# Low parts of split operands computed on VectorE instead of GpSimd, with a new table of priorities, in an attention and two feed-forward layers

## The chip, the core and the metric

The kernel runs on one core of a Trainium2 chip. A core has a matrix engine (PE), a vector engine (DVE), a scalar engine (ACT), a general engine (POOL) and a queue engine (SP) that issues transfers. Each engine executes its own list of instructions strictly in the order in which the program wrote them; between engines, semaphores carry the dependences. The metric is the device time of one execution in microseconds (us).

## What is computed

Attention with a memory term over 4 batches of 8 heads, 576 rows and 64 columns a head, then two feed-forward layers over the 2304 resulting rows, all in fp32:

```
scores = scale * q @ k.T, causal; a = softmax(scores); local = a @ v
q_p = phi(q); mem_out = (q_p @ M_prev) / (q_p @ z_prev + 1e-6)
x = g * mem_out + (1 - g) * local            # 2304 x 512
h = x @ w_in;  x = (h * tanh(softplus(h))) @ w_out    # 512 -> 2048 -> 512
h = x @ w_in2; out = (h * sigmoid(h)) @ w_out2        # 512 -> 2048 -> 512
```

## The kernel before

**Attention.** Two heads make a pair; 16 pairs follow one another, with some overlap. For a pair DVE takes scores out of PSUM with a mask and a row minimum (L562), ACT takes the exponential (L586), DVE adds a constant to the row sums and inverts them (L616 and L618, two elements a partition), POOL scales the rows (L601, L619), PE transposes them (L638, L655) and multiplies them with the values (L674), and ACT writes the result into `xT`, which holds all of x with features on partitions (`Vc`, recorded under L481).

**Feed-forward.** Rows go in 6 tiles `t` of 384, the 2048 hidden columns in 16 slices `i` of 128, in 4 groups of 4 slices. One unit is (layer, t, i); there are 192. For a unit PE does 12 matmuls into `hp` (L843 to L845; below, the *in* part), ACT applies the activation (L858) and rounds the result to `gh` (L859), DVE takes the rest `gl = a - gh` (L860), and PE does the *out* part into `acc` (L880; 12 matmuls of 384 columns in layer 0, 9 of 512 in layer 1). After each group of four slices `acc` is added into `xT` (L895 on ACT, L897 on DVE).

**Split operands.** Each fp32 operand of these matmuls is a rounded high part and a low part, original minus high. The high part of x is `xh`, made by ACT (L826); the low part `xl` is made by `lo()` of `split_x` (L829), 4 instructions a tile: 24 in layer 0, 24 in layer 1. A weight slice arrives in `stg` (two buffers); DVE extracts its value in five steps (L761, L769, L771, L773, L776), ACT rounds it (L784) and `s_lo` makes the low part (L788) and frees the `stg` buffer. There are 64 such weight jobs; the 8 of the first group are worked off while attention still runs, the last of them at its end. Before, POOL makes all 64 weight low parts and 46 of the 48 `xl`; DVE makes the other two.

**What sets the order.** The program gives a planner (`Steps.plan`) each step with its engine, an assumed duration and its dependences. The planner works out a latest start for each, adds the sum of the entries of the table `SHIFT` that fit the step, and lists the steps of each engine by walking through an assumed schedule. PE, DVE, ACT, POOL and SP then follow these lists. `PERIOD` spaces the pairs in that schedule. Buffers are rings: 3 banks for `hp`, 5 for `acc`, 3 buffers each for `a`, `gh`, `gl`.

Of the kernel before, what the change touches and what calls it, by code (L numbers as in the profile page):

```python
# [721 lines left out]
GC = NF // NG  # L722
# [5 lines left out]
class Weights:  # L728
# [13 lines left out]
    def steps(self, n):  # L742
        job = self.jobs[n]
        ph, i, part = job
        nc = self.nc

        def s_load():
            t = self.stg.tile([P, DM, 2], I32, tag="stg", name="stg")
            src = self.pairs[ph][part].bitcast(I32)
            if part == 0:  # L750
                nc.sync.dma_start(
                    t.rearrange("p (c f) x -> p c (f x)", c=KC),
                    src[:, 2 * i * P:2 * (i + 1) * P].rearrange("(c p) f -> p c f", p=P))
            else:
                nc.sync.dma_start(t.rearrange("p f x -> p (f x)"), src[i * P:(i + 1) * P, :])
            self.raw[job] = t

        def s_abs():
            c = self.stg.tile([P, DM], F32, tag="val", name="val", bufs=self.VALS)
            self.val[job] = c  # L760
            nc.vector.tensor_scalar(  # L761
                c.bitcast(U32), self.raw[job][:, :, 1].bitcast(U32), 0x7FFFFFFF, None, op0=ALU.bitwise_and)

        def s_bits(n):
            t, c = self.raw[job], self.val[job]
            cu = c.bitcast(U32)
            lo, hi = t[:, :, 0].bitcast(U32), t[:, :, 1].bitcast(U32)
            if n == 0:
                nc.vector.tensor_scalar(c, c, LEAST, MOST, op0=ALU.max, op1=ALU.min)  # L769
            elif n == 1:  # L770
                nc.vector.tensor_scalar(cu, cu, 3, 0x3FFFFFFF, op0=ALU.logical_shift_left, op1=ALU.bitwise_and)  # L771
            elif n == 2:
                nc.vector.scalar_tensor_tensor(  # L773
                    out=cu, in0=lo, scalar=29, in1=cu, op0=ALU.logical_shift_right, op1=ALU.bitwise_or)
            else:
                nc.vector.scalar_tensor_tensor(  # L776
                    out=lo, in0=hi, scalar=0xC0000000, in1=cu, op0=ALU.bitwise_and, op1=ALU.bitwise_or)

        def s_hi():
            k = i % SLOTS  # L780
            pool = self.fix if k < GC else self.late
            w = pool.tile([P, 2, DM], F32R, tag=f"w{k}{part}", name=f"w{k}{part}")
            self.W[job] = w
            nc.scalar.copy(w[:, 0, :], self.raw[job][:, :, 0].bitcast(F32))  # L784

        def s_lo():
            w = self.W[job]
            nc.gpsimd.tensor_tensor(  # L788
                w[:, 1, :], self.raw[job][:, :, 0].bitcast(F32), w[:, 0, :].bitcast(F32), op=ALU.subtract)
        bits = {f"b{n}": lambda n=n: s_bits(n) for n in range(4)}  # L790
        return dict(ld=s_load, abs=s_abs, hi=s_hi, lo=s_lo, **bits)

    def register(self, m, due, last):

        m.cap.update({"W.raw": 2, "W.val": self.VALS})
        for n, job in enumerate(self.jobs):
            ph, i, part = job
            f = self.steps(n)
            k = i % SLOTS
            ring = f"W.{k}{part}"  # L800
            m.cap[ring] = 1
            J = lambda x: ("W", job, x)
            t = due(job)
            slow = 0.2 if ph == 0 and i < GC else 0.0
            for x, e, d, deps in (("ld", "S", 3.8, []), ("abs", "D", 0.465, ["ld"]), ("b0", "D", 0.465, ["abs"]),
                                  ("b1", "D", 0.465, ["b0"]), ("b2", "D", 0.735, ["b1"]), ("b3", "D", 0.78, ["b2"]),
                                  ("hi", "A", 0.57, ["b3"] + (["open1"] if k >= GC else [])),
                                  ("lo", "G", 1.38, ["hi"])):
                m.add(J(x), e, d + (slow if e == "D" else 0.0), [y if y == "open1" else J(y) for y in deps], f[x], t)
            m.hold("W.raw", job, [J("ld")], [J("lo")], order=n)  # L810
            m.hold("W.val", job, [J("abs")], [J("b3")], order=n)
            m.hold(ring, job, [J("hi")], last(job), order=n)


class Moe:
# [5 lines left out]
    def split_x(self, ph, t, kc):  # L821
        nc = self.nc
        ts = slice(t * TB, (t + 1) * TB)

        def hi():
            nc.scalar.copy(self.xh[t][:, kc], self.xT[:, kc, ts])  # L826

        def lo():
            self.lo_engine(ph, t, kc).tensor_tensor(  # L829
                self.xl[t][:, kc], self.xT[:, kc, ts], self.xh[t][:, kc].bitcast(F32), op=ALU.subtract)  # L830
        return hi, lo

# [67 lines left out]
        r = t * TB + d * P  # L900
        self.nc.sync.dma_start(self.out[r:r + P, :], self.part(1, t, d))

    def lo_engine(self, ph, t, kc):
        return self.nc.vector if ph == 0 and t == 0 and kc % 2 else self.nc.gpsimd

    def open(self, n):

        tc, ctx = self.tc, self.ctx
# [17 lines left out]
    def register(self, m, base, ends, step=4.17):  # L926
# [6 lines left out]
        for t in range(NB):  # L933
            for kc in range(KC):
                k = ("x", t, kc)
                f = self.split_x(0, t, kc)
                heads = [(b * KC + kc, v) for b in range(t * TB // SEQ, ((t + 1) * TB - 1) // SEQ + 1) for v in ends]
                m.add((k, "h"), "A", 0.413, ["open%d" % (t // 3)] + heads, f[0], due[0, t, 0])
                e = self.lo_engine(0, t, kc) is self.nc.gpsimd
                m.add((k, "l"), "G" if e else "D", 0.955 if e else 0.466, [(k, "h")], f[1], due[0, t, 0])  # L940
        for n, u in enumerate(U):
            ph, t, i = u
            g = i // GC
# [26 lines left out]
            if i % GC == GC - 1:  # L970
                for d in range(nd):
# [11 lines left out]
                    if g == NG - 1 and ph == 0:  # L983
                        f = self.split_x(1, t, d)
                        z = ("z", t, d)
                        m.add((z, "h"), "A", 0.413, [k], f[0], due[1, t, 0])
                        m.add((z, "l"), "G", 0.955, [(z, "h")], f[1], due[1, t, 0])
                    elif g == NG - 1:
                        m.add((k, "st"), "S", 0.5, [k], lambda t=t, d=d: self.store(t, d), due[u] + 4)

# [10 lines left out]
        self.w.register(m, wdue, wlast)  # L1001


PERIOD = 9.921
SHIFT = {
# [19 lines left out]
}  # L1025


# [75 lines left out]
```

## Time and profile before

| | |
|---|---|
| median of 3 runs | 1046.67 us (1046.45 to 1046.94) |
| profiled execution, its own time | 1046.64 us |
| its span, first to last instruction | 1044.8 us |
| PE, share of the span busy | 97% |
| DVE | 56% |
| ACT | 44% |
| POOL | 28% |

The profiled time is within 0.03 us of the median, and 1.84 us of it lie outside the span. A busy PE in this profile is not PE at its peak: matmuls overlap, and one row of 0.33 us follows the one before it after 0.17 us. So idle time of PE alone undercounts what a stall costs, and the pace (how far apart the rows start) is the better measure.

### The profile page before, as it was taken

The page shows a single profiled execution, that of the slowest core. Times are in us where ns is not written, and L with a number is a line of the kernel's source. Part 1 is how long each engine was busy: PE and PEld are TensorE (multiplying, and loading weights), DVE is VectorE, ACT ScalarE, POOL GpSimd, SP SyncE. Part 2 cuts the span into 40 slices and gives each one's busy share as a digit, 9 for nine tenths or more (in the row PEclk, how much of TensorE's full clock was granted, in tenths as well). Part 3 has the DMA queues.
Part 4 walks back from the last instruction along what each step waited for, and adds up shares of the span by engine and source line. Part 5 has one row for each costly group of instructions (what it writes and reads, how often), then busy time and mean ns, then how long its engine had stood idle before and what let it go on. Part 6 is the DMA issues. An engine that isn't in the chain of part 4 may idle for free.

```text
span 1044.8 us, 15751 instructions
## 1 busy us (share of the span) xinstructions
PE 1015.3 (97%) x5824; PEld 902.3 (86%) x5824; DVE 584.3 (56%) x1398; ACT 461.5 (44%) x1071; POOL 291.6 (28%) x303
## 2 busy tenths in 40 slices
PE   6999999988999999999999999999999999999998
PEld 4666666677999999999999999899999999998897
DVE  6999999999724732672278238512752372212222
ACT  6899898983424322332234334324422332222221
POOL 4887778787201200210024234101200120000000
PEclk9999999999999999999999999999999999999999
DMA  6433343122302300220031002100300120000011
GB/s 135 101 92 82 92 102 93 46 67 68 102 1 61 101 1 1 82 81 1 1 101 61 1 21 81 61 1 21 118 24 1 41 81 1 1 1 31 31 61 61
DMA packets 85309, 55.03 MB, mean 53 GB/s; under 512 B 61936, under 2 KB 78320, under 8 KB 85232
## 3 DMA queue, kind: packets, MB, share of 16 engines
q1 hardware_dynamic: 84032, 53.73, 18.2%
q8 instruction: 46, 0.75, 0.3%
q10 hardware_dynamic: 1200, 0.30, 0.1%
q14 instruction: 31, 0.25, 0.1%
HBM read 49.29 MB, written 4.72 MB: 52 GB/s over the span
## 4 chain that ended last, share of the span: by engine, by line
PE 80%; DVE 10%; POOL 4%; ACT 3%; issue 2%; DMA 1%; SPq 0%; POOLq 0%; ACTq 0%; DVEq 0%
PE acc L880 37%; PE hp L843 12%; PE hp L844 12%; PE hp L845 12%; DVE sm L562 3%; POOL xl L829 2%; PE ps_x L674 2%; PE ps_s L569 2%; DVE h L484 2%; ACT P L586 2%; PE ps_t L638 1%; DVE z L616 1%; DVE e L513 1%; PE ps_t L489 1%; DMA nq<-in_q_dram 1%
## 5 line engine op out<-in xcount | busy, mean ns | idle before, releaser
L858 ACT ACTIVATE a<-hp 128x384 f32<-128x384 f32 x192 | 94.5, 492 | 469.5 <-PE hp L845 469.4
L860 DVE TENSOR_TENSOR gl<-a,gh 128x384 fp32r<-128x384 f32 x192 | 116.4, 606 | 320.6 <-ACT gh L859 320.1
L843 PE MATMUL hp<-xh,w 128*128 128x384 f32 x768 | 258.9, 337 | 0.0
L844 PE MATMUL hp<-xl,w 128*128 128x384 f32 x768 | 258.5, 337 | 0.0
L845 PE MATMUL hp<-xh,w 128*128 128x384 f32 x768 | 258.5, 337 | 0.0
L788 POOL TENSOR_TENSOR w<-stg,w 128x512 fp32r<-128x512 f32 x64 | 86.6, 1354 | 474.5 <-ACT w L784 341.1
L880 PE MATMUL acc<-gh,w 128*128 128x384 f32 x768 | 212.1, 337 | 1.5 <-ACT gh L859 1.5
L880 PE MATMUL acc<-w,gh 128*128 128x512 f32 x576 | 180.4, 394 | 0.0
L843 PEld LDWEIGHTS hp<-xh,w 128*128 128x128 f32 x768 | 144.2, 188 | 4.5 <-issue 0.3
L844 PEld LDWEIGHTS hp<-xl,w 128*128 128x128 f32 x768 | 144.2, 188 | 4.2 <-DVE xl L829 0.2
L845 PEld LDWEIGHTS hp<-xh,w 128*128 128x128 f32 x768 | 144.2, 188 | 0.0
L880 PEld LDWEIGHTS acc<-gh,w 128*128 128x128 f32 x768 | 140.6, 188 | 1.8 <-ACT gh L859 1.8
L880 PE MATMUL acc<-gl,w 128*128 128x384 f32 x384 | 130.2, 339 | 7.0 <-DVE gl L860 7.0
L880 PEld LDWEIGHTS acc<-w,gh 128*128 128x128 f32 x576 | 106.9, 188 | 17.4
L897 DVE TENSOR_TENSOR xT<-acc,xT 128x384 f32<-128x384 f32 (+1 forms) x126 | 73.9, 612 | 83.6 <-PE acc L880 83.6
L880 PE MATMUL acc<-w,gl 128*128 128x512 f32 x288 | 113.8, 395 | 0.2 <-DVE gl L860 0.2
L601 POOL TENSOR_SCALAR P<-P,z,g 128x448 f32<-128x448 f32 (+3 forms) x128 | 94.0, 746 | 31.1 <-DVE z L618 17.3
L859 ACT CAST gh<-a 128x384 fp32r<-128x384 f32 x192 | 98.6, 513 | 5.4
L586 ACT ACTIVATE P<-sm,m 128x576 f32<-128x576 f32 (+4 forms) x144 | 83.7, 583 | 8.8 <-DVE m L562 6.7
L880 PEld LDWEIGHTS acc<-gl,w 128*128 128x128 f32 x384 | 72.1, 188 | 9.5 <-DVE gl L860 9.4
L784 ACT CAST w<-stg 128x512 fp32r<-128x512 f32 x64 | 42.3, 661 | 68.9 <-DVE stg L776 62.3
L880 PEld LDWEIGHTS acc<-w,gl 128*128 128x128 f32 x288 | 54.1, 188 | 14.0 <-DVE gl L860 1.4
(80 smaller groups left out, 1131.2 us busy)
## 6 DMA issues: line engine op xcount, KB each, us to landing
stg<-in_moe_w_in_dram SPq DMA_DIRECT2D x32, 512.0 KB, 3.7
stg<-in_moe_w_out_dram SPq DMA_DIRECT2D x32, 512.0 KB, 3.5
out_dram<-xT SPq DMA_DIRECT2D x18, 256.0 KB, 2.0
nq<-in_q_dram SPq DMA_DIRECT2D x32, 128.0 KB, 2.6
nv<-in_v_dram SPq DMA_DIRECT2D x32, 128.0 KB, 2.7
nk<-in_k_dram SPq DMA_DIRECT2D x30, 128.0 KB, 2.7
z<-in_z_prev_dram SPq DMA_DIRECT2D x4, 256.0 KB, 4.4
nq<-in_q_dram SPq DMA_DIRECT2D x16, 32.0 KB, 2.5
```

The source lines that it names most:

```text
L586: nc.scalar.activation(G(f"P{i}")[:, 1 - j if i else 1], s[f"sm{i}{j}"], AF.Exp, bias=s[f"m{i}"][:, j:j + 1], scale=-1.0, accum_out=G(f"z{ ...
L601: f[f"n{i}{j}"] = lambda i=i, j=j: nc.gpsimd.tensor_scalar(s[f"P{i}"][:, 1 - j], s[f"P{i}"][:, 1 - j], s[f"z{i}"][:, j:j + 1], self.g1[:, ...
L784: nc.scalar.copy(w[:, 0, :], self.raw[job][:, :, 0].bitcast(F32))
L788: nc.gpsimd.tensor_tensor(w[:, 1, :], self.raw[job][:, :, 0].bitcast(F32), w[:, 0, :].bitcast(F32), op=ALU.subtract)
L843: nc.tensor.matmul(hp, lhsT=wh, rhs=xh, start=(kc == 0), stop=False)
L844: nc.tensor.matmul(hp, lhsT=wh, rhs=xl, start=False, stop=False)
L845: nc.tensor.matmul(hp, lhsT=wl, rhs=xh, start=False, stop=(kc == KC - 1))
L858: f["si"] = lambda: nc.scalar.activation(self.new(u, "a", TB), self.hp[u], fn)
L859: f["gh"] = lambda: nc.scalar.copy(self.new(u, "gh", TB, F32R), g("a"))
L860: f["gl"] = lambda: nc.vector.tensor_tensor(self.new(u, "gl", TB, F32R), g("a"), g("gh").bitcast(F32), op=ALU.subtract)
L880: nc.tensor.matmul(o, lhsT=a, rhs=b, start=(first and k == 0), stop=(last and k == 2))
L897: nc.vector.tensor_tensor(part, acc, part, op=ALU.add)
```

## The change

Three things. Every `xl` is computed by DVE (`lo_engine` is gone). `s_lo` runs on POOL only for the first group of layer 0 (8 jobs), on DVE for the other 56. The planner is told so, with 0.466 and 0.6 as the assumed durations on DVE. The table of priorities is another one, and has entries for classes of steps that had none: the parts of a feed-forward unit by layer (`M`), the drains (`dr`), the weights by group (`Wg`) and by group, slice and part (`Wj`), and the second layer's splits (`z`). No instruction is added or dropped.

```
         def s_lo():
             w = self.W[job]
-            nc.gpsimd.tensor_tensor(
+            eng = nc.gpsimd if ph == 0 and i < GC else nc.vector
+            eng.tensor_tensor(
                 w[:, 1, :], self.raw[job][:, :, 0].bitcast(F32), w[:, 0, :].bitcast(F32), op=ALU.subtract)
...
         def lo():
-            self.lo_engine(ph, t, kc).tensor_tensor(
+            nc.vector.tensor_tensor(
                 self.xl[t][:, kc], self.xT[:, kc, ts], self.xh[t][:, kc].bitcast(F32), op=ALU.subtract)
...
-    def lo_engine(self, ph, t, kc):
-        return self.nc.vector if ph == 0 and t == 0 and kc % 2 else self.nc.gpsimd
...
-PERIOD = 9.921
+PERIOD = 10.582
 SHIFT = {
-    ('a', 'ldnk'): 25.36, ('a', 'ldnv'): 49.95, ('a', 'phe'): -177.34, ('a', 'phu'): -13.77, ('a', 'Tk'): 18.81,
...
+    ('a', 'ldnk'): 30.28, ('a', 'ldnv'): 61.83, ('a', 'phe'): -269.17, ('a', 'phu'): -0.59, ('a', 'Tk'): 15.94,
...
```

How the lists change is shown at three places. In the names, `w_...` is a weight slice, `xl_...` the low part of one tile of rows, `P_...` a score block; numbers differ between the two programs.

POOL, at the end of attention, before; `w_3532` is the sixth of the first group's eight weight slices, `w_3627` and `w_3707` the seventh and eighth, `w_3781` the first of the next group:

```order
L788 TENSOR_TENSOR w_3532<-stg,w_3532 128x512
L601 TENSOR_SCALAR P_3446<-P_3446,z_3447,g_105 128x320
L829 TENSOR_TENSOR xl_3588<-xT,xh_3587 128x384 x2
L788 TENSOR_TENSOR w_3627<-stg,w_3627 128x512
L829 TENSOR_TENSOR xl_3590<-xT,xh_3589 128x384 x4
L829 TENSOR_TENSOR xl_3592<-xT,xh_3591 128x384
L788 TENSOR_TENSOR w_3707<-stg,w_3707 128x512
L829 TENSOR_TENSOR xl_3592<-xT,xh_3591 128x384 x3
L829 TENSOR_TENSOR xl_3685<-xT,xh_3684 128x384
L788 TENSOR_TENSOR w_3781<-stg,w_3781 128x512
```

The same place in the changed program, down to POOL's last computing instruction:

```order
L789 TENSOR_TENSOR w_3528<-stg,w_3528 128x512
L619 TENSOR_SCALAR P_3504<-P_3504,z_3505,g1s 128x128
L601 TENSOR_SCALAR P_3472<-P_3472,z_3473,g_105 128x192
L601 TENSOR_SCALAR P_3437<-P_3437,z_3438,g_105 128x320
L789 TENSOR_TENSOR w_3652<-stg,w_3652 128x512
L789 TENSOR_TENSOR w_3752<-stg,w_3752 128x512
```

POOL's list ends with the last two weight slices of the first group; all `xl` and all later weight slices are gone from it.

DVE, where the feed-forward begins, before, from the last steps of attention's end to the second `gl`:

```order
L829 TENSOR_TENSOR xl_3588<-xT,xh_3587 128x384
L769 TENSOR_SCALAR val<-val 128x512
L771 TENSOR_SCALAR val<-val 128x512
L773 SCALAR_TENSOR_TENSOR val<-stg,val 128x512
L776 SCALAR_TENSOR_TENSOR stg<-stg,val 128x512
L761 TENSOR_SCALAR val<-stg 128x512
L860 TENSOR_TENSOR gl<-a,gh 128x384
L769 TENSOR_SCALAR val<-val 128x512
L771 TENSOR_SCALAR val<-val 128x512
L860 TENSOR_TENSOR gl<-a,gh 128x384
```

The changed program, around its first three `gl`:

```order
L773 SCALAR_TENSOR_TENSOR val<-stg,val 128x512
L830 TENSOR_TENSOR xl_3678<-xT,xh_3677 128x384
L776 SCALAR_TENSOR_TENSOR stg<-stg,val 128x512
L830 TENSOR_TENSOR xl_3678<-xT,xh_3677 128x384 x3
L761 TENSOR_SCALAR val<-stg 128x512
L830 TENSOR_TENSOR xl_3680<-xT,xh_3679 128x384
L861 TENSOR_TENSOR gl<-a,gh 128x384 x3
L769 TENSOR_SCALAR val<-val 128x512
L830 TENSOR_TENSOR xl_3680<-xT,xh_3679 128x384
L771 TENSOR_SCALAR val<-val 128x512
L830 TENSOR_TENSOR xl_3680<-xT,xh_3679 128x384 x2
```

The `xl` now stand between the weight steps; 17 of the first layer's 24 come ahead of the first `gl`, which itself comes after more of the weight work than before.

PE, at the first out part, before; `w_3162` is the third slice for the *in* part of the first tile, `w_1663` the first slice for the *out* part:

```order
L845 MATMUL hp<-xh_3587,w_3162 128x384
L880 MATMUL acc<-gh,w_1663 128x384
L880 MATMUL acc<-gl,w_1663 128x384
L880 MATMUL acc<-gh,w_1663 128x384 x2
```

The changed program at its first out part; `xh_3588` is the second tile of rows, `w_2247` the second slice, `w_1661` the first slice for the *out* part:

```order
L846 MATMUL hp<-xh_3588,w_2247 128x384
L881 MATMUL acc<-gh,w_1661 128x384
L881 MATMUL acc<-gl,w_1661 128x384
L881 MATMUL acc<-gh,w_1661 128x384 x2
```

Before, PE's list has three *in* parts, two *out* parts, and then alternates, so that one unit is in hand between its *in* and its *out* part. Changed, it has six *in* parts, three *out* parts, and then alternates with three units in hand, from the second half of the first layer on with two.

## Rows read from the trace of the kernel before

**Rows 1.** The page, part 1: busy us, share of the span, instructions.

```profile
PE 1015.3 (97%) x5824; PEld 902.3 (86%) x5824; DVE 584.3 (56%) x1398; ACT 461.5 (44%) x1071; POOL 291.6 (28%) x303
```

**Rows 2.** Busy time by stretch: length, busy us (instructions) by engine, clock, DMA.

```profile
25.00:222.00 197.00, 189.30 (x1413) 125.01 (x1411) 189.37 (x720) 176.78 (x500) 149.59 (x174) 1.00 0.36 86
...
230.40:270.00 39.60, 31.12 (x169) 29.04 (x169) 35.72 (x39) 18.33 (x41) 26.66 (x21) 1.00 0.26 79
...
300.00:650.00 350.00, 350.00 (x1997) 348.48 (x1995) 177.08 (x295) 118.29 (x232) 65.95 (x53) 1.00 0.14 44
```

**Rows 3.** The chain that ended last, from 222 us: start, us, what.

```profile
225.08 5.07 POOL xl L829 x4
...
272.24 2.08 PE acc L880 x12
```

**Rows 4.** PE in time order: the first feed-forward matmuls, and the last.

```profile
222.11 0.45 PE L843 MATMUL hp<-xh,w 128*128 128x384 f32 x1
...
223.38 0.76 PE L674 MATMUL ps_x<-W,MV 128*64 128x320 f32 x4
...
224.72 0.44 PE L843 MATMUL hp<-xh,w 128*128 128x384 f32 x1
...
1040.78 0.40 PE L880 MATMUL acc<-w,gl 128*128 128x512 f32 x1
```

**Rows 5.** PE's matmuls from 222 to 272.2 us by form: count, busy, mean ns.

```profile
L880 PE MATMUL acc<-gh,w 128*128 128x384 f32 x65 | 17.9, 337 | 1.5 <-ACT gh L859 1.5
L843 PE MATMUL hp<-xh,w 128*128 128x384 f32 x40 | 13.6, 340 | 0.0
...
L880 PE MATMUL acc<-gl,w 128*128 128x384 f32 x32 | 11.5, 358 | 7.0 <-DVE gl L860 7.0
```

**Rows 6.** PE's weight loads from 222 to 272 us: who waited for whom, us, times, longest.

```profile
PEld acc L880 <- DVE gl L860: 9.1, 7, 2.9
PEld acc L880 <- ACT gh L859: 1.8, 1, 1.8
```

**Rows 7.** The same from 272 us to the end.

```profile
PEld acc L880 <- DVE gl L860: 1.7, 4, 0.6
```

**Rows 8.** DVE in time order, 219 to 270 us: start, duration, instruction.

```profile
219.62 1.38 DVE L776 SCALAR_TENSOR_TENSOR stg<-stg,val 128x512 uint32<-128x512 uint32 x1
220.92 0.68 DVE L484 COPY h<-ps_t 128x512 f32<-128x512 f32 x1
221.52 1.26 DVE L829 TENSOR_TENSOR xl<-xT,xh 128x384 fp32r<-128x384 f32 x1
...
263.14 0.43 DVE L771 TENSOR_SCALAR val<-val 128x512 uint32<-128x512 uint32 x1
263.60 0.69 DVE L773 SCALAR_TENSOR_TENSOR val<-stg,val 128x512 uint32<-128x512 uint32 x1
264.40 0.69 DVE L776 SCALAR_TENSOR_TENSOR stg<-stg,val 128x512 uint32<-128x512 uint32 x1
...
267.38 0.55 DVE L860 TENSOR_TENSOR gl<-a,gh 128x384 fp32r<-128x384 f32 x1
267.85 0.41 DVE L769 TENSOR_SCALAR val<-val 128x512 f32<-128x512 f32 x1
```

**Rows 9.** `gl` from 230 to 265 us, then from 300 to 400: min/median/max ns.

```profile
L860 DVE TENSOR_TENSOR gl<-a,gh x7: 546/1342/1371, 231.8 to 261.9; 128x384 fp32r<-128x384 f32 x7
...
L860 DVE TENSOR_TENSOR gl<-a,gh x24: 548/558/1367, 303.2 to 399.1; 128x384 fp32r<-128x384 f32 x24
```

**Rows 10.** `xl`: two on POOL in time order; POOL's from 222 to 262 us; DVE's two.

```profile
219.15 1.30 POOL L829 TENSOR_TENSOR xl<-xT,xh 128x384 fp32r<-128x384 f32 x1
221.36 1.01 POOL L829 TENSOR_TENSOR xl<-xT,xh 128x384 fp32r<-128x384 f32 x1 [0.91 <-ACT xh L826]
...
L829 POOL TENSOR_TENSOR xl<-xT,xh 128x384 fp32r<-128x384 f32 x21 | 25.9, 1262 | 0.9 <-ACT xh L826 0.9
...
L829 DVE TENSOR_TENSOR xl<-xT,xh 128x384 fp32r<-128x384 f32 x2 | 2.6, 1318 | 0.0
```

**Rows 11.** Attention's additions to the row sums, 25 to 222 us, ns and totals.

```profile
L616 DVE TENSOR_SCALAR z<-z x74: 107/162/1527, 26.4 to 213.7; 128x2 f32<-128x2 f32 x60, 128x1 f32<-128x1 f32 x14
...
L616 DVE TENSOR_SCALAR z<-z 128x2 f32<-128x2 f32 (+1 forms) x74 | 21.8, 296 | 2.5 <-ACT P L586 2.0
```

More of the change, by code (lines that the diff above doesn't have):

```diff
@@ L807, in register @@
                                   ("hi", "A", 0.57, ["b3"] + (["open1"] if k >= GC else [])),
-                                  ("lo", "G", 1.38, ["hi"])):
+                                  ("lo",) + (("G", 1.38) if ph == 0 and i < GC else ("D", 0.6)) + (["hi"],)):
                 m.add(J(x), e, d + (slow if e == "D" else 0.0), [y if y == "open1" else J(y) for y in deps], f[x], t)
@@ L938, in register @@
                 m.add((k, "h"), "A", 0.413, ["open%d" % (t // 3)] + heads, f[0], due[0, t, 0])
-                e = self.lo_engine(0, t, kc) is self.nc.gpsimd
-                m.add((k, "l"), "G" if e else "D", 0.955 if e else 0.466, [(k, "h")], f[1], due[0, t, 0])
+                m.add((k, "l"), "D", 0.466, [(k, "h")], f[1], due[0, t, 0])
         for n, u in enumerate(U):
@@ L986, in register @@
                         m.add((z, "h"), "A", 0.413, [k], f[0], due[1, t, 0])
-                        m.add((z, "l"), "G", 0.955, [(z, "h")], f[1], due[1, t, 0])
+                        m.add((z, "l"), "D", 0.466, [(z, "h")], f[1], due[1, t, 0])
                     elif g == NG - 1:
```

57 rows, old and new, of the table SHIFT are left out of this document.

## Prediction

> **What bounds the kernel now.** I read the page's busy shares first [rows 1]: PE is at 97%, so only the stretches in which PE is not fed can give anything. The busy times by stretch [rows 2] show where: in the feed-forwards (300 to 650 us) PE is busy all the time while DVE has half of it free; from 230.4 to 270 us PE works only 31.12 of 39.60 us, with DVE at 35.72; in attention (25 to 222 us) PE and DVE are both at 96%. The chain of waits [rows 3] runs through POOL's `xl` (the row at 225.08 us is the first of several such) and from 272.24 us, where the row stands for all that follow, through PE alone. So the place of this change is 222 to 270 us, where attention hands over to the feed-forward. Everything behind it is PE at its pace, and a microsecond saved there is a microsecond at the end.
>
> What the handover costs is read from PE's pace. From the first feed-forward matmul at 222.11 [rows 4] to 272.24 [rows 3] PE did 10 *in* parts (40 matmuls of L843, four a part) and 8 *out* parts (64 with `gh` and 32 with `gl`, twelve a part; the 65th opens the next) [rows 5]. Undisturbed, a part takes 2.08 us (the row at 272.24 [rows 3]), and attention's last product in between takes 224.72 - 223.38 = 1.34 us [rows 4]. That makes 18 x 2.08 + 1.34 = 38.8 us; it took 50.1. So 11.3 us were lost. The waits of PE's weight loads give nearly the same, with names: 9.1 us for DVE's `gl`, 1.8 us for ACT's `gh`, together 10.9 [rows 6]. I use 10.9.
>
> Why `gl` is late there: DVE is slowed. The same instruction takes 1.342 us at the median in that stretch and 0.558 us later [rows 9]; L776 takes 1.38 us at 219.62, while POOL makes an `xl` (219.15 to 220.45), and 0.69 us at 264.40, with none on POOL [rows 8, 10]. 21 `xl` on POOL, 1.262 us each [rows 10], thus hold back about as many DVE instructions by 0.7 to 0.8 us each.
>
> **The change part by part.**
>
> *The first layer's `xl` (22 more on DVE, all in the handover).* The price of one on DVE without POOL beside it is not in the trace. The two DVE rows have 1.318 us [rows 10], but the one shown (221.52, 1.26 us [rows 8]) stands beside a POOL `xl` (from 221.36). Same engine, operation, shape and types are in `gl` at 267.38: 0.55 us, the next instruction 0.47 us after it [rows 8]. I take 0.47; the bounds are 0.47 and 1.26. On DVE the whole list from the seventh weight slice's last step (L776) to the first `gl` is: 17 `xl`, one copy of 0.6, four weight steps of 0.46, one of 0.80, one of 0.7 [rows 8]: 8.0 + 0.6 + 1.8 + 0.8 + 0.7 = 11.9 us. POOL still makes one weight slice in that time: one collision, 1.38 - 0.69 = 0.7. It begins where L484 begins at 220.92 [rows 8], less the 0.7 that L776 lost there to a POOL `xl` that is gone: 220.2. So the first `gl` can start at about 232.8. PE, from 222.11, has six *in* parts ahead of its first *out* part: 222.11 + 1.34 + 6 x 2.08 = 235.9. `gl` is there 3 us before it is wanted. Before, three *in* parts stood ahead, so by its pace PE would have come to its first *out* part at 229.7, and the first `gl` began at 231.8 [rows 9].
>
> The first matmul needs the first two `xl`: 220.2 + 2 x 0.47 = 221.1, ahead of 222.11. I credit no earlier start; that could be up to 1 us. What stays lost: the split first unit, and short waits for ACT, which has all of the 24 roundings `xh` earlier in its list than before. Between 0.3 and 3 us; I take 0.8, since each single wait for ACT now is at most 1.8 and the buffers of `hp` cover three units. **Handover: -10.9 + 0.8 = -10.1 us.**
>
> *The 56 weight low parts and the second layer's 24 `xl` on DVE.* 56 x about 0.7 (the weight form is 512 columns wide; L773 with two inputs of that width takes 0.69) + 24 x 0.55 = 52 us more on DVE, spread over 770 us, where DVE is idle about half the time [rows 2]. They lie beside PE's work. The cost if that cover is gone: a low part stands right behind its own last step L776 in places, so DVE waits for ACT's rounding, under 1 us, with `gl` queued behind it, and PE waits for `gl`. PE now has two or three units in hand, 8 to 12 us, so I cost it at nothing. The load of the weight slice after next is issued when a low part is done; on SP nothing stands behind it that PE waits for. Two of these loads also move behind the transfers of an attention pair; at nothing, for weight slices are wanted long after. In return the collisions with POOL end here too: of the 1.7 us that weight loads still wait for `gl` after 272 us [rows 7] I take back 1.3. **Feed-forwards: -1.3 us** (0 to -1.7; +2 if DVE's in-order waits reach PE now and then).
>
> *The new priorities in attention.* The same instructions on the same engines, in another order for about half of them. POOL's work there is the same. Both lists have six of the first group's weight slices begun on DVE before the last score block. What the order can change is how often DVE runs into POOL: the 74 additions to row sums take 0.162 us at the median and 0.296 on average, up to 1.527 [rows 11], which makes 21.8 - 74 x 0.162 = 9.8 us of collisions. DVE is at 96% there, so most of it counts. I see nothing that moves this one way; I take 0, with 4 us (40% of those 9.8) to either side.
>
> *The tail* (last drain, last store) is the same on all engines: 0.
>
> **Sum:** 1046.64 (the profiled execution, 0.03 below the median) - 10.1 - 1.3 + 0 = 1035.2 us, 1.1% faster.
>
> **The rivals.**
>
> *A. An `xl` on DVE costs 1.26 us with POOL idle too.* Then 17 x (1.26 - 0.47) = 13.4 us come on DVE ahead of the first `gl`: 232.8 + 13.4 = 246.2, against 235.9, so PE waits 10.3 us, and the total is 1035.2 + 10.3 = 1045.5: no change. For it speaks that the only two DVE rows have that price; against it that `gl`, the same form, takes 0.55 as soon as POOL is quiet. The Trainium skill points this way: its page "Perfetto Trace Analysis", section "Optimizing Scalar/DVE Operations", says that DVE and POOL share a read port, so moving work between the two might not help. Followed to the letter it would leave the handover as it is, about 1046 us. The rows do not bear it out: per `xl` POOL's 1.262 us stand against 0.55 on DVE. Chance 4%.
>
> *B. Attention gets slower by more than the handover wins.* One mechanism: DVE's additions to row sums, or POOL's scalings, meet each other more often. A full hit costs 1.527 - 0.162 = 1.37 us; the 9.8 us are about 7 such hits in 197 us. To be slower than before by 0.2% (2.1 us) the new order needs (11.4 + 2.1) / 1.37, about 10 more hits, all on the path: 17 instead of 7. It would end near 1049. Chance 4%. A part of that, 4 to 9 us, gives 1040 to 1044.5, still faster: 11%.
>
> *C. Attention gets faster* by the same mechanism, more than 4 us: below 1031. Chance 9%.
>
> *D. The change does not do what it says* (low parts still on POOL): the lists exclude it; POOL's ends with attention.
>
> **How the numbers follow.** The forecast, 1031 to 1040, has 72%, A 4%, B 4%, its milder form 11%, C 9%. The predicted time is 1035.2. The range, 1030.5 to 1042.5, takes in the bounds of the handover (2.2 above, 0.5 below, 1 for an earlier start) and of attention (4 either way); about 7% lie below it and 13% above. About 0.2%, or 2.1 us, is what a measurement of this kernel tells from no change: faster 92% (forecast, milder B, C), same 4% (A), slower 4% (B).
>
> **What would show it.** In the changed profile: POOL has no row behind attention's end, and its busy time falls from 291.6 us by over 100; `xl` on DVE has a mean near 0.6, and `gl` a median near 0.56 from 225 to 270 us too; PE's weight loads wait about 1 us instead of 10.9 in the 50 us behind the first feed-forward matmul; that matmul starts within 4 us of 222.1; from there PE keeps its parts 2.08 us apart at once. The first matmul's start tells attention's share, the distance from there to the last matmul (818.7 us before [rows 4]) the handover's and the feed-forwards'; that distance should be about 807. I am wrong if the distance shrinks by much less than 11 us (A, or waits of DVE for ACT), or if the start moves by more than 4 us (B or C).

## The result, and the profile after

The changed kernel takes **1033.15 us** (median of 4 runs, 1033.11 to 1033.78) against 1046.8 us beside it: ratio **0.987**, 95% interval [0.985, 0.989]. The prediction was 1035.2 us with a range of 1030.5 to 1042.5; the time is 2 us below the forecast and inside the range. The profiled execution took 1033.11 us.

The first look is at the busy shares and at the stretches that [rows 1] and [rows 2] showed of before (stretch, length, then busy us with instructions of PE, its weight loads, DVE, ACT and POOL, then the granted clock, the share of the DMA engines and GB/s):

```profile
PE 1010.8 (98%) x5824; PEld 901.8 (87%) x5824; DVE 584.1 (57%) x1500; ACT 461.1 (45%) x1071; POOL 160.7 (16%) x201
```

```profile
25.00:222.00 197.00, 189.10 (x1420) 124.49 (x1420) 189.23 (x724) 178.58 (x505) 146.30 (x172) 1.00 0.37 86
222.00:272.00 50.00, 50.00 (x293) 49.42 (x290) 42.22 (x84) 29.40 (x62) 3.08 (x2) 1.00 0.28 89
230.40:270.00 39.60, 39.60 (x230) 39.60 (x229) 32.04 (x64) 20.52 (x43) 1.32 (x1) 1.00 0.29 93
300.00:650.00 350.00, 350.00 (x1990) 348.04 (x1990) 192.39 (x363) 119.47 (x235) 0.00 (x0) 1.00 0.15 47
```

DVE has 102 instructions more and yet the same busy time (584.1 us, before 584.3): what 102 more rows cost it, the rows that POOL no longer holds up gave back. From 230.4 to 270 us PE works 39.60 of 39.60 us, before 31.12. The rows of PE's weight loads that waited for `gl` and `gh` [rows 6, 7] have no counterpart: not one such wait is left.

PE in time order gives the two parts of the account (first feed-forward matmul, the first *out* part, the last matmul; start, duration):

```profile
220.39 0.42 PE L844 MATMUL hp<-xh,w 128*128 128x384 f32 x1
...
234.64 0.33 PE L881 MATMUL acc<-gh,w 128*128 128x384 f32 x1
234.81 0.33 PE L881 MATMUL acc<-gl,w 128*128 128x384 f32 x1
...
1027.24 0.40 PE L881 MATMUL acc<-w,gl 128*128 128x512 f32 x1
```

Against [rows 4] the first matmul comes 222.11 - 220.39 = **1.72 us earlier** (attention's share), and the distance from it to the last one falls from 818.67 to 806.85 us, by **11.82 us** (handover and feed-forwards). I call these two numbers *start* and *distance* from here on. Behind the first *out* part the chain of waits holds PE alone, with twelve matmuls in the undisturbed 2.08 us from the start:

```profile
234.80 6.24 PE acc L881 x36
...
243.12 2.08 PE acc L881 x12
```

DVE at the handover, in time order, answers [rows 8], and the two groups of `gl` (min/median/max ns) answer [rows 9]:

```profile
218.91 1.54 DVE L830 TENSOR_TENSOR xl<-xT,xh 128x384 fp32r<-128x384 f32 x3
...
222.89 0.55 DVE L830 TENSOR_TENSOR xl<-xT,xh 128x384 fp32r<-128x384 f32 x1
223.36 1.55 DVE L771 TENSOR_SCALAR val<-val 128x512 uint32<-128x512 uint32 x1
...
231.06 0.55 DVE L830 TENSOR_TENSOR xl<-xT,xh 128x384 fp32r<-128x384 f32 x1
233.28 1.50 DVE L861 TENSOR_TENSOR gl<-a,gh 128x384 fp32r<-128x384 f32 x3 [1.67 <-ACT gh L860]
```

```profile
L861 DVE TENSOR_TENSOR gl<-a,gh x11: 551/558/559, 233.3 to 262.8; 128x384 fp32r<-128x384 f32 x11
L861 DVE TENSOR_TENSOR gl<-a,gh x179: 548/558/561, 275.1 to 1022.4; 128x384 fp32r<-128x384 f32 x179
```

An `xl` takes 0.55 us on DVE; one row at 223.36 stands beside a POOL row and takes 1.55 instead of 0.42. Two weight slices are all that POOL still makes behind the first feed-forward matmul (the 3.08 us of the second stretch above). The first `gl` waited 1.67 us, not for DVE but for ACT's `gh`.

Attention's additions to the row sums [rows 11] took 18.7 us, 3.1 less than before:

```profile
L616 DVE TENSOR_SCALAR z<-z 128x2 f32<-128x2 f32 (+1 forms) x74 | 18.7, 255 | 1.2 <-ACT P L586 0.8
```

### The profile page after: what moved, and what is told of

Its sections match the earlier page's. It is cut to its first block, busy times and chain, and to the rows that moved or that the text cites. A ratio compares the mean times of both kernels' runs of the same rounds, so it can differ in the third digit from the quotient of the medians.

```text
span 1031.3 us, 15634 instructions
## 1 busy us (share of the span) xinstructions
PE 1010.8 (98%) x5824; PEld 901.8 (87%) x5824; DVE 584.1 (57%) x1500; ACT 461.1 (45%) x1071; POOL 160.7 (16%) x201
## 4 chain that ended last, share of the span: by engine, by line
PE 88%; DVE 8%; ACT 2%; DMA 1%; POOL 1%; issue 1%; SPq 0%; ACTq 0%; POOLq 0%
PE acc L881 39%; PE hp L844 13%; PE hp L846 13%; PE hp L845 13%; PE ps_x L674 3%; PE ps_s L569 3%; PE ps_t L638 2%; DVE sm L562 2%; DVE h L484 2%; PE ps_t L489 1%; DVE z L616 1%; ACT P L586 1%; DMA nq<-in_q_dram 1%; DVE e L513 1%; POOL P L601 1%
## 5 line engine op out<-in xcount | busy, mean ns | idle before, releaser
L861 DVE TENSOR_TENSOR gl<-a,gh 128x384 fp32r<-128x384 f32 x192 | 106.8, 557 | 308.4 <-ACT gh L860 307.1
L601 POOL TENSOR_SCALAR P<-P,z,g 128x576 f32<-128x576 f32 (+3 forms) x128 | 93.2, 739 | 36.8 <-ACT P L586 8.1
L586 ACT ACTIVATE P<-sm,m 128x448 f32<-128x448 f32 (+4 forms) x144 | 83.8, 584 | 6.7 <-DVE m L562 5.3
L638 PEld LDWEIGHTS ps_t<-ident,P 128*128 128x128 f32 x384 | 41.5, 141 | 25.3 <-POOL P L601 6.2
L569 PE MATMUL ps_s<-kT,qT 64*128 64x288 f32 (+3 forms) x320 | 62.8, 473 | 0.4 <-DVE m L562 0.3
```

Of the source, the lines that this page charges most:

```text
L569: nc.tensor.matmul(ps, lhsT=s["qT"][R[j], qcols(i)], rhs=s["kT"][R[j], k0 + cols.start:k0 + cols.stop], start=True, stop=True)
L586: nc.scalar.activation(G(f"P{i}")[:, 1 - j if i else 1], s[f"sm{i}{j}"], AF.Exp, bias=s[f"m{i}"][:, j:j + 1], scale=-1.0, accum_out=G(f"z{ ...
L601: f[f"n{i}{j}"] = lambda i=i, j=j: nc.gpsimd.tensor_scalar(s[f"P{i}"][:, 1 - j], s[f"P{i}"][:, 1 - j], s[f"z{i}"][:, j:j + 1], self.g1[:, ...
L638: nc.tensor.transpose(ps[:, o:o + P], src, self.ident)
L861: f["gl"] = lambda: nc.vector.tensor_tensor(self.new(u, "gl", TB, F32R), g("a"), g("gh").bitcast(F32), op=ALU.subtract)
```

## Experiments

Two theories stood against each other. **Theory 1:** DVE was slowed by POOL's rows beside it; take them away and `gl` is in time, the units that PE has in hand being a reserve. **Rival 2:** the new order, with three units in hand instead of one, is the gain, and which engine makes the low parts matters little. A second pair concerns attention: **theory B**, that the row-sum additions and their collisions lie on its path, against the view that PE or the list sets its pace. Lists are those of before or after, as each edit says. All were compared with the kernel before, which took 1046.8 to 1047.0 us at the median beside them.

### The engines without the new priorities

```
-PERIOD = 10.582
+PERIOD = 9.921
 SHIFT = {
-    ...            # the new table
+    ...            # the table of before
```

> The changed kernel's engines with the table of priorities and the period of before: PE's list again has three in parts ahead of its first out part and one unit in hand. Theory 1 (what made PE wait was that POOL's low parts slowed DVE; the units in hand are a reserve that is hardly drawn on): almost all of the gain between the first feed-forward matmul and the last stays, their distance is 807 to 809 us (818.7 before, 806.9 changed), and the time is 1035 to 1037 us, the rest being the later start. Rival 2 (the units in hand, so the table, made the gain): the distance is 815 us or more, the time 1043 or more.

Measured: 1035.87 us (1035.64 to 1035.91), ratio 0.990 [0.988, 0.991]. Start 222.28, distance 807.73. PE has three *in* parts and two *out* parts ahead of the alternation, as before: one unit in hand. This is all that waits for `gl` or `gh` behind it:

```profile
PEld acc L881 <- DVE gl L861: 1.2, 1, 1.2
```

The change of engines alone brings 10.94 of the 11.82 us of distance and nothing of the start. The new table brings the other 0.88 us and the whole of the start.

### The new lists with POOL's `xl`

```
+            eng = nc.gpsimd if ph == 0 and not (t == 0 and kc % 2) else nc.vector
-            nc.vector.tensor_tensor(
+            eng.tensor_tensor(
                 self.xl[t][:, kc], ...
```

> The changed kernel with every list as it is, except that the first layer's 22 low parts of x that POOL made before are made by POOL again, each at its place in the program's order. PE keeps six in parts ahead and three units in hand. Theory 1: DVE is slowed again in the handover, gl takes 1.3 us there, PE waits 5 to 10 us for gl, time 1038 to 1043 us. Rival 2: the three units in hand cover DVE's slowness, gl still takes 1.3 us but PE waits under 2 us, time 1033 to 1035.5 us.

Measured: 1039.12 us (1038.54 to 1040.08), ratio 0.993 [0.991, 0.994]. Start 220.60, distance 812.07: 5.2 us worse than after, but 6.6 better than before. PE's weight loads from 216 to 272 us, and ACT in time order at the stall:

```profile
PEld acc L882 <- ACT xT L897: 3.6, 1, 3.6
...
PEld acc L882 <- DVE gl L862: 0.3, 1, 0.3
```

```profile
251.55 0.66 ACT L784 CAST w<-stg 128x512 fp32r<-128x512 f32 x1 [6.37 <-DVE stg L776]
252.10 0.86 ACT L897 COPY xT<-acc 128x384 f32<-128x384 f32 x2
```

The time fell into theory 1's range, but not by the wait it names. Three units in hand did cover `gl`: 0.3 us instead of 9.1. The slowed DVE reached PE another way: ACT stood 6.37 us in front of a weight rounding whose last step was late on DVE, and the drain that PE needed to get its `acc` bank back stood behind it in ACT's list. Both theories hold a part: 6.6 us are gained although POOL makes the first layer's `xl`. That is the new lists together with the weights' low parts and the second layer's `xl`, which stay on DVE here; how much of it is the lists alone no run shows, for none has the new lists with all of POOL's rows.

### The old lists with the first layer's `xl` on DVE

```
-            self.lo_engine(ph, t, kc).tensor_tensor(
+            (nc.vector if ph == 0 else nc.gpsimd).tensor_tensor(
```

> The kernel before with every list as it is, except that the first layer's 22 low parts of x on POOL go to DVE, each at its place in the program's order. PE has one unit in hand as before. Theory 1: gl takes 0.56 us in the handover, PE's weight loads wait 1 to 3 us there instead of 10.9, time 1036 to 1039 us. Rival 2: DVE is free of collisions, but with one unit in hand PE still waits 7 us or more, time 1043 us or more.

Measured: 1039.39 us (1039.06 to 1039.81), ratio 0.993 [0.992, 0.995], a little above theory 1's range. Start 222.10, distance 810.66: these 22 instructions alone bring 8.0 us. Left are 3.4 us of waits for `gl` in the handover and 1.3 behind it, since POOL still makes the weights' low parts and PE has one unit in hand.

### The weights' low parts on POOL, all 64

```
-            eng = nc.gpsimd if ph == 0 and i < GC else nc.vector
+            eng = nc.gpsimd
```

> The changed kernel, with all 64 low parts of weights on POOL at their places in the lists (before the change that engine made them too); the low parts of x stay on DVE. It asks what the 56 low parts of weights contribute by themselves. Theory 1 (once the low parts of x are off POOL, PE has three units in hand and a lone collision of DVE with POOL is covered): no weight load of PE waits for gl after the first out part, gl still has single rows near 1.3 us, 1033 to 1034.2 us. Rival 2 (each collision that is left reaches PE through an engine's list): 1034.5 to 1036 us, with waits of 1 to 3 us in all at PE's weight loads behind the handover.

Measured: 1033.51 us (1032.88 to 1033.83), ratio 0.987 [0.986, 0.989], as theory 1 expected. Start 220.90, distance 806.85, which is after's to the hundredth. Single rows of `gl` still take 1.35 us in the handover and up to 1.43 later (median 0.56), and none makes PE wait. So moving 56 of the 64 low parts of weights brought nothing here. With one unit in hand the same rows on POOL cost 810.66 - 807.73 = 2.9 us; that comparison also moves the second layer's `xl`, and the planner's lists with them.

### One unit in hand, by a ring of two in the planner

```
-        m.cap.update({"M.h": 3, "M.y": 5})
+        m.cap.update({"M.h": 3, "M.y": 5, "M.hand": 2})
...
+            m.hold("M.hand", u, [N("in") if n else N("in0")], outs, order=n)
```

> The changed kernel with one more rule for the planner: at most two units between their in and their out part, so that PE's list is two in parts, then alternating, with one unit in hand; engines and table as changed. Theory 1 as it stands in the prediction's sum has DVE's first gl behind 17 low parts and the weight steps: gl ready near 231 to 232 us, while PE would come to its first out part at 220.4 + 1.3 + 4.2 = 226 us; so 5 to 6 us lost once at the start of the feed-forward and under 1 us after, time 1037.5 to 1040 us. Rival 2: a loss of 8 us or more, spread over several units, 1041 us or more. If one unit in hand is enough: 1033 to 1034.5.

Measured: 1042.60 us (1041.93 to 1042.88), ratio 0.996 [0.995, 0.997]; theory 1 missed, the time lies where rival 2 put it. Start 221.09, distance 815.60. The waits, and the stretches around them (PE, its weight loads, DVE, ACT, POOL, clock):

```profile
PEld acc L881 <- ACT gh L860: 6.8, 1, 6.8
PEld acc L881 <- DVE gl L861: 0.7, 1, 0.7
```

```profile
226.00:232.00 6.00, 1.09 (x7) 0.77 (x5) 5.83 (x13) 5.97 (x13) 0.00 (x0) 0.94 0.30 87
232.00:236.00 4.00, 2.14 (x6) 1.75 (x7) 2.44 (x5) 1.94 (x5) 1.30 (x1) 0.50 0.08 23
236.00:240.00 4.00, 4.00 (x19) 4.00 (x19) 4.00 (x10) 0.68 (x1) 0.00 (x0) 0.73 0.28 113
```

PE did not wait for `gl` but for `gh`. ACT was busy 5.97 of 6.00 us: the changed priorities put eight roundings `xh` and a weight rounding between the activation and its `gh`. So this run does not price a missing unit in hand; it shows what happens when ACT's list is not in step with PE's. The price of one unit in hand with an ACT list that fits is the first experiment's 0.88 us. Of the 8.75 us of distance lost here the two waits make 7.5; the clock fell too, of which more below.

### A twin of each `xl` on POOL

```
+            if ph == 0:
+                nc.gpsimd.tensor_tensor(
+                    self.twin[t // 3], self.xT[:, kc, ts], self.xh[t][:, kc].bitcast(F32), op=ALU.subtract)
             nc.vector.tensor_tensor(
                 self.xl[t][:, kc], ...
```

> The changed kernel, and for each of the first layer's xl also a twin of it on POOL, which writes a buffer that nobody reads (24 POOL instructions more; the output is that of the changed kernel). No data comes later by the twins themselves, so it prices POOL's presence beside DVE alone. Theory 1 (DVE is slowed by POOL's row, not late by waiting for POOL's results): DVE's rows beside the twins take about 1.3 us instead of 0.55 to 0.7, some 20 of them before the first gl, which comes near 245 us instead of 233; PE stalls of 8 us or more, 1041 to 1048 us. Rival 2 (what cost time before was DVE and PE waiting for POOL's results, not the slowed rows): at most 1036 us.

Measured: 1047.96 us (1047.56 to 1048.86), ratio 1.001 [1.000, 1.002]: the top of theory 1's range, and the whole gain gone, by 24 instructions whose results nobody reads. DVE, then POOL, in time order (the last number of a row is the count of instructions in it), then `xl` (min/median/max ns):

```profile
231.22 7.79 DVE L833 TENSOR_TENSOR xl<-xT,xh 128x384 fp32r<-128x384 f32 x6
238.93 1.48 DVE L773 SCALAR_TENSOR_TENSOR val<-stg,val 128x512 uint32<-128x512 uint32 x1
240.33 0.55 DVE L833 TENSOR_TENSOR xl<-xT,xh 128x384 fp32r<-128x384 f32 x1
240.80 0.68 DVE L776 SCALAR_TENSOR_TENSOR stg<-stg,val 128x512 uint32<-128x512 uint32 x1
```

```profile
226.07 13.79 POOL L831 TENSOR_TENSOR twin<-xT,xh 128x384 f32<-128x384 f32 x11
242.25 1.32 POOL L789 TENSOR_TENSOR w<-stg,w 128x512 fp32r<-128x512 f32 x1 [2.39 <-ACT w L784]
```

```profile
L833 DVE TENSOR_TENSOR xl<-xT,xh x24: 543/1349/1647, 219.7 to 260.9; 128x384 fp32r<-128x384 f32 x24
```

Up to 239.86 POOL runs its twins, and an `xl` costs DVE 7.79 / 6 = 1.30 us. From there to 242.25 POOL is idle, and at once the next `xl` takes 0.55 and L776 takes 0.68. POOL's own rows take 13.79 / 11 = 1.25 us: while both work, DVE does about one instruction to each of POOL's. The first `gl` comes at 246.3 instead of 233.3. PE's waits from 205 to 272 us:

```profile
PEld acc L884 <- ACT gh L863: 6.9, 1, 6.9
PEld acc L884 <- DVE gl L864: 4.0, 1, 4.0
```

The longer of the two goes back to DVE as well: ACT had stood 8.36 us in front of a weight rounding that needed DVE's L776, and `gh` stood behind it in ACT's list:

```profile
241.51 0.66 ACT L784 CAST w<-stg 128x512 fp32r<-128x512 f32 x1 [8.36 <-DVE stg L776]
```

With 1.2 us for `xl` these waits make 12.1 of the 14.4 us by which the distance grew. The granted clock stood at 0.50 from 242 to 250 us, behind the stall; whether the rest is the clock's no run separates.

### The first group's weights on DVE too

```
-            eng = nc.gpsimd if ph == 0 and i < GC else nc.vector
+            eng = nc.vector
```

> The changed kernel, with the first group's 8 low parts of weights on DVE too, at their places: POOL then makes only attention's rows. Theory 1: the collision at 223 us goes, which the units in hand cover already, and attention's DVE list gets some six rows of 0.7 us against six collisions fewer: no difference, 1032.3 to 1034 us. Rival 2 (in attention DVE bounds and the rows add to it): 1035 to 1038 us, by a first feed-forward matmul 2 to 5 us later.

Measured: 1035.45 us (1034.41 to 1036.66), ratio 0.989 [0.988, 0.991]; my expectation fell, and the median lies in rival 2's range. The profiled execution, which took 1036.35 us, has a distance of 806.98, unchanged, and a start of 223.48, 3.1 us later. In attention the six low parts that fall there add 4.4 us to DVE, more than came back by collisions that went (DVE is busy 190.54 us from 25 us to the start, after 187.86):

```profile
L789 DVE TENSOR_TENSOR w<-stg,w 128x512 fp32r<-128x512 f32 x6 | 4.4, 730 | 0.0
```

The four executions spread more than after's: 1034.41, 1034.55, 1036.35 and 1036.66 us, so the loss is 1.3 to 3.5 us, and the two shorter ones lie between the two ranges. The profiled one also had a lower granted clock early on (0.60 from 15 to 20 us and 0.72 from 20 to 25, after 0.68 and 0.98); how much of the 3.1 us is owed to that stays open. All four are longer than all of after's: there, where DVE is busy 96% of the time, POOL is the better place for these rows.

### Without the row-sum additions

```
-            f[f"a{i}"] = lambda i=i, n=n: nc.vector.tensor_scalar(
-                s[f"z{i}"][:, :n], s[f"z{i}"][:, :n], 1.0, 1e-9, op0=ALU.mult, op1=ALU.add)
+            f[f"a{i}"] = None
```

Three kernels: the changed one, the changed one with the table of before, and the kernel before, each with this edit.

> The changed kernel without the 80 small additions to the row sums on DVE (L616; 1e-9 added to sums that are at least 1, which float32 does not hold; this part of the computation is left out). They take 18.7 us of DVE's time in attention, collisions with POOL among it. Theory B (the milder rival of the prediction: DVE's row-sum additions lie on attention's path): the first feed-forward matmul moves from 220.4 to 203 to 215 us and the total to 1016 to 1028 us. Rival (PE, at 96% of that stretch, or the order of the list sets the pace): the start moves by less than 4 us, 1029.5 to 1033 us.

> The changed kernel's engines with the old lists, and without the 80 row-sum additions of L616 (that part of the computation is left out). The new lists start the feed-forward 1.7 to 1.9 us earlier than the old ones; this asks whether by the additions' collisions (22.1 us of them by the old lists, 18.7 by the new). Theory B (by the collisions): without the additions both lists start alike, within 1 us of 213.9, and the time is 1026 to 1029 us. Rival (the lists differ in other ways): it starts 1.5 to 3 us behind that, at 215.4 to 217, 1028.5 to 1031 us.

> The kernel before, with its lists and its engines, without the 80 row-sum additions of L616 (that part of the computation is left out). It asks whether attention and the handover are two separate accounts. Theory (separate): the first feed-forward matmul comes 6 to 8 us earlier than 222.1, the distance to the last matmul stays at 817.5 to 820 us, 1038.5 to 1041.5 us in all. Rival (what attention gains is lost to an earlier but worse handover): the distance grows by 2 us or more, 1042 us or more.

Measured, in us:

| | time | ratio | start | distance |
|---|---|---|---|---|
| before | 1046.8 | | 222.11 | 818.67 |
| before, no additions | 1038.41 (1038.32 to 1038.63) | 0.992 [0.990, 0.994] | 213.95 | 818.43 |
| old table, new engines | 1035.87 | 0.990 [0.988, 0.991] | 222.28 | 807.73 |
| the same, no additions | 1027.80 (1027.41 to 1029.17) | 0.982 [0.981, 0.983] | 213.62 | 807.86 |
| after | 1033.15 | 0.987 [0.985, 0.989] | 220.39 | 806.85 |
| after, no additions | 1026.83 (1026.68 to 1026.93) | 0.981 [0.979, 0.982] | 213.90 | 806.98 |

Theory B holds in all three. Without the additions the three starts agree within 0.33 us, whichever table and engines: the new table's 1.7 us in attention came by less time in these small additions (18.7 us of them instead of 21.8), for without them it is gone. Of the additions 12 take over 0.4 us in either kernel, each of them beside a POOL row; 0.9 us or more take 7 before and 4 after. The distances stay within 0.24 us of those with the additions, so start and distance are two accounts that can be added. The kernel before without the additions came 0.1 us below the range of its theory, with the start 0.2 us further than expected.

In attention PE then works more of each microsecond (after, then after without the additions, the same stretch ahead of both first feed-forward matmuls):

```profile
25.00:213.90 188.90, 181.00 (x1353) 118.78 (x1353) 181.51 (x711) 171.59 (x487) 143.12 (x168) 1.00 0.37 87
25.00:213.90 188.90, 185.31 (x1410) 122.74 (x1408) 176.00 (x645) 175.50 (x500) 145.86 (x172) 1.00 0.37 90
```

The last row of the table beats both kernels. What it leaves out does no work: a row sum contains the exponential of the row's own extreme (L562 takes it, L586 subtracts it), which is 1, so the sum is at least 1, and 1e-9 added to it is lost in fp32.

## Why the prediction was right, point by point

**The bound and the place.** PE behind the handover, as read from [rows 2, 3]: what was saved there is a microsecond at the end, 11.82 of distance and 1.72 of start make 13.54, and the profiled execution became 13.53 us shorter.

**Handover and feed-forwards, -11.4 forecast, -11.82 measured.** The step "DVE is slowed by POOL's rows" is shown from both sides: with POOL's rows gone and the old order the distance falls by 10.94; with useless POOL rows put back it rises by 14.4 us to 821.3. The terms:
- An `xl` on DVE was taken at 0.47 a step; in the changed trace three take 1.54 us, and the row is 0.55. Rival A (1.26 with POOL idle) falls: POOL idle, it is 0.55 in the twin kernel too, microseconds behind rows of 1.30. The Trainium skill, page "Perfetto Trace Analysis", section "Optimizing Scalar/DVE Operations", warns that moving work between these two engines might not help since they share a read port. The trace agrees with the sharing (1.30 beside POOL, 0.55 without) and not with the warning: the move was worth 10.94 us here, because DVE, which got the work, had paid 0.75 us a row for the sharing.
- The first `gl` was put at 232.8 and came at 233.28, but not by my count: DVE had nothing to do for 1.67 us and waited for `gh`. I had priced ACT at short waits of PE; it came within a microsecond of being the bound, since PE began its first *out* part at 234.64. The reserve was about 1 us, not 3. That ACT's list is the next one to break shows in the runs with the ring and with POOL's `xl`, where PE waited 6.8 and 3.6 us for ACT, and with the twins, 6.9 us.
- "0.8 stays lost": from 220.39 to 234.64 are 14.25 us, against 1.34 + 6 x 2.08 = 13.82; 0.43 stayed.
- The moved weights (-1.3) came out, but my reason is only one of two that suffice. With all of them on POOL and three units in hand nothing waits; with them on DVE and one unit in hand nothing waits behind the handover either. In the changed kernel the move is worth nothing that can be measured (1033.51 against 1033.15 us, overlapping).
- Three units in hand were costed as cover. That is what they are. The new lists that bring them are worth 0.88 us with POOL quiet and 3.8 with the weights on POOL (810.66 to 806.85; the second layer's `xl` move too). With the first layer's `xl` on POOL only their sum with the weights' move is known, 6.6 us.

**Attention, 0 forecast with 4 to either side, -1.72 measured.** This is the term that was mis-sized, and with it the sum: 1046.64 - 11.82 - 1.72. The mechanism named, the additions' hits on POOL rows, is the right one, as the starts without additions show; it was the time of the hits that fell, not the number of rows hit. What I could not read from the trace of before was its sign. The size that rivals B and C rested on, that most of a collision counts, is borne out in part: the additions as a whole (18.7 to 22.1 us busy) are worth 6.5 to 8.7 us of start, more than a third.

**What would show it.** One sign did not come as written: POOL was to have no row behind attention's end, and it has two, the last at 232.08. The others came: POOL has 130.9 us less, `xl` 0.55, `gl` 0.558 in the handover too, no weight load waiting, the start moved by less than 4 us, the distance at 807.

## What to carry to other kernels

Two engines that hold each other up are best read from one instruction form at two places, once with the other engine busy and once idle; the price of an instruction on the second engine is what it takes from the first. Units of work in hand and fewer collisions are two cures for the same wait, and their gains do not add up: fewer collisions alone brought 10.94 of the 11.82 us and the units in hand then 0.88 more; the new lists with the first layer's `xl` on POOL brought 6.6, and quiet on POOL then 5.2 more. A row of two elements a partition can cost as much as a large one if it stands in an in-order list beside such an engine, so the first thing to ask of it is whether it is needed.

## What the runs showed of the hardware

**DVE beside POOL.** Rows of two elements can suffer as large ones do: the additions take 0.158 us at the median and 1.453 at the most in the changed kernel. The longest of the kernel before ends within 0.03 us of the POOL row beside it:

```profile
88.47 1.53 DVE L616 TENSOR_SCALAR z<-z 128x2 f32<-128x2 f32 x1
88.42 1.55 POOL L515 TENSOR_TENSOR u<-e,z 128x640 f32<-128x640 f32 x1
```

But not every small row is held up. The reciprocals of the same two elements (L618) stand in the same stretch of the same trace, where POOL is busy 149.59 of 197 us, and none takes over 0.167 us:

```profile
L618 DVE RECIPROCAL z<-z x75: 103/154/167, 25.0 to 213.9; 128x2 f32<-128x2 f32 x61, 128x1 f32<-128x1 f32 x14
```

With the additions left out, when they no longer stand right behind one, it is 0.167 us at the most again. So it is the operation that decides here, not the size alone. Of the additions, all twelve over 0.4 us are of two elements; none of the 14 of a single element [rows 11] is among them. The Trainium skill, page "SBUF — State Buffer", section "Who interferes with whom", says that a DVE instruction with two inputs in SBUF contends with POOL's reads, and one with a single input does not outside the two-port modes. The twin's rows agree with the first (one instruction of DVE to each of POOL's, 1.30 and 1.25 us). The additions and the reciprocals both have a single input; the reciprocals fit the second, and in which mode the additions run no run here shows.

**PE's clock after a pause.** In the run with the ring PE stood still in its wait of 6.8 us, and the granted clock then read 0.50 from 232 to 236 us and 0.73 from 236 to 240: the lower level (1.2 GHz), then the upper (2.4 GHz) again. The length of the pause alone does not tell. The kernel before has PE at 1.60 of 4 us from 230 to 234, and keeps its clock:

```profile
230.00:234.00 4.00, 1.60 (x8) 1.03 (x7) 3.30 (x4) 3.27 (x8) 2.69 (x4) 1.00 0.09 11
234.00:238.00 4.00, 2.79 (x17) 2.47 (x16) 3.96 (x4) 2.26 (x6) 3.63 (x4) 1.00 0.36 126
```

The same program without the additions has the same stretch 8 us earlier, with PE at 1.58, and loses it:

```profile
222.00:226.00 4.00, 1.58 (x8) 1.01 (x8) 3.28 (x4) 3.33 (x8) 2.67 (x4) 1.00 0.08 11
226.00:230.00 4.00, 3.83 (x14) 3.33 (x13) 3.97 (x4) 2.21 (x6) 3.58 (x4) 0.57 0.36 124
```

In 3.83 busy us it does 14 matmuls there, in 2.79 us 17 before. It happens once more behind its next long pause, where the kernel before did 24 matmuls at a clock of 1.00 (254 to 258 us):

```profile
246.00:250.00 4.00, 4.00 (x16) 4.00 (x15) 3.96 (x4) 0.76 (x2) 4.00 (x4) 0.58 0.37 117
```

The two stretches lack (0.43 + 0.42) x 4 = 3.4 us of the upper clock. PE's waits for `gl` and `gh` are 9.2 us in all (6.0 and 1.8 in the handover, 1.4 later) against 12.6 in [rows 6, 7], 3.4 us less, and yet the distance is the same within 0.24. The slower clock did not lengthen this handover, for DVE set its pace: from the first `gl` (223.78 us, before 231.83) to the sixth every one starts 8.04 to 8.08 us earlier than before, at either clock. The sixth, before and without the additions:

```profile
256.68 1.37 DVE L860 TENSOR_TENSOR gl<-a,gh 128x384 fp32r<-128x384 f32 x1
248.60 1.35 DVE L859 TENSOR_TENSOR gl<-a,gh 128x384 fp32r<-128x384 f32 x1
```

So PE only came later to data that was late anyway, and its waits shrank by what the clock took. Where PE is itself the bound, the clock can cost time: in the run with the ring it did 19 matmuls from 236 to 240 us, busy throughout, where after does 25. Why one pause drops the clock and the other not stays open; it is not the program alone, for the executions of the kernel before have mean granted clocks from 0.993 to 0.998. What follows for a reader of waits: a shorter sum of waits need not be a gain, and the distance is what counts.
